# Seven block products for eight: Strassen's algorithm in the last block of a transformer layer

## The chip, the cores and the metric

The kernel runs on one core of a Trainium2 chip. The time is that of one execution on the device in microseconds. Comparisons use the median of several runs; before the change it is 1405.76 us (three runs, 1405.62 to 1406.48).

## The reference: what is computed

One pre-norm transformer layer on 2048 tokens of 512 features, in float32: attention with 32 query heads of 16 features that share one key and one value head, then a gated feed-forward part with 1792 hidden features.

```python
h  = x + A(layernorm(x))        # q = x@wq, k = x@wk, v = x@wv; softmax(q k^T / 4) v, all heads; @ wo
h2 = h + (gelu(n @ w_gate) * (n @ w_up)) @ w_down      # n = layernorm(h)
```

The change concerns the two products `n @ w_gate` and `n @ w_up`, each 512 x 512 by 512 x 1792 for a block of 512 tokens.

## The kernel before, in words

**Blocks and chunks.** The tokens are four blocks of 512 (`NB`, `T`). A block's dense part (`dense`) is the output projection, the layer norm, the feed-forward part and the residual sums. The hidden features are 14 chunks of 128 (`FC`). The dense part of block b runs between the attention steps of block b + 1 (`weave`, steps of the kind "woven"); that of the last block has no attention left beside it and runs alone, by `tail`, at the end. This last stretch is where most of the change lies.

**High and low parts.** TensorE multiplies in a format that keeps fewer bits than float32 (`F32R`). So each operand is split into a high part and a low rest (`split`: one copy, one subtraction), and each product is three matmuls: high by high, high by low, low by high. The split weights are made once, at the start of the kernel, by GpSimd (`part_weights`) and kept in device memory (`w1_d`, `w2_d`); a load of one chunk of `w_gate` or `w_up` brings both parts, 512 KB (`load_w1`), into one of `W1` buffers. Loads of `w_down` for two chunks are 1 MB (`load_w2`) and go to a ring of three.

**The last block.** `start_tail` makes the normalised input, transposed by TensorE (`x_turn`), as `xT_hi` and `xT_lo` (tiles `x2h`, `x2l`). For each chunk `up` runs 12 matmuls of 512 columns for the gate (`pg`) and 12 for the other factor (`pu`). VectorE evicts them and makes square and cubic term (`leave_gate`: tiles `g`, `ga`), ScalarE does the tanh (`gate`), VectorE multiplies and splits the result into `gh` and `gl`. After four chunks, `down` multiplies them by `w_down` for four token tiles of 128 (`pd`, 12 matmuls each) and VectorE adds each into `h` (`add_down`). Two chunks lie between the fourth chunk and its down product:

```python
RUNS = ((0, 1, 2, 3), (4, 5, 6, 7), (8, 9, 10, 11), (12, 13))
```

**What sets the order.** Every engine works through its own instructions in order. In the last stretch TensorE, ScalarE and GpSimd keep the order in which the code issues them; a scheduler places those of VectorE and the DMAs of the SP queue, once, when the program is built. An instruction waits for the semaphores of those it depends on, and all behind it on its engine wait too.

Of the kernel before, what the change touches and what calls it, by code (L numbers as in the profile page):

```python
# [9 lines left out]
F32 = mybir.dt.float32  # L10
# [9 lines left out]
P = 128  # L20
# [5 lines left out]
BOUND_PAD = 1.02  # L26
PB = 5

W1 = 6

W2 = 3

# [35 lines left out]
def kernel(  # L68
# [104 lines left out]
    def run(outer, first):  # L173
# [10 lines left out]
        def psum1(name):  # L184
            return ps.tile([P, T], F32, tag="d", bufs=width, name=name)
# [282 lines left out]
                step()  # L468

        def evacuate(b, g, acc):  # L470
            oT = sb.tile([P, T], F32, tag="oT", bufs=2, name=f"oT_{b}_{g}")
            nc.vector.tensor_copy(oT, acc)  # L472
            c, k = divmod(g, 2)
            last = b == NB - 1 and g == NG - 1
# [72 lines left out]
        def part_weights(pw):  # L547
# [53 lines left out]
                yield 1  # L601
            left()

        def load_w1(b, i):
# [53 lines left out]

        tail_ps = None

        def tail_bank(name):
# [12 lines left out]
        def dense(b, tail=False):  # L674
# [13 lines left out]
            w1 = {i: load_w1(b, i) for i in range(W1)}  # L688
            if b == 0:
                yield 0  # L690
            w2 = {}
# [16 lines left out]

            def x_turn(t):

                bank = tail_bank if tail and t != 2 else psum1
                pt = bank(f"pxt_{b}_{t}").rearrange("p (c q) -> p c q", c=DC)
                for c in range(DC):
                    nc.tensor.transpose(pt[:, c, :], xns[t][:, c * P : (c + 1) * P], ident)  # L714
# [32 lines left out]

            def start_tail():

                xp, xn, h = (  # L750
                    sb.tile([P, TB, D], F32, tag="p", bufs=PB, name=f"{n}p_{b}")
                    for n in ("x", "xn", "h")
                )
                for t in range(TB):
                    nc.sync.dma_start(xp[:, t, :], x_t[:, b * TB + t, :])
# [2 lines left out]
                nc.gpsimd.tensor_copy(one, ident)  # L758
                xh = sb.tile([P, TB, D], F32R, tag="p", bufs=PB, name=f"xhp_{b}")
                xl = sb.tile([P, TB, D], F32R, tag="p", bufs=PB, name=f"xlp_{b}")  # L760
                for t in range(TB):
# [61 lines left out]
            gs, g_of = {}, {}  # L823

            def next_w1(i):
                if i + W1 < 2 * FC:
                    w1[i + W1] = load_w1(b, i + W1)

            def leave_gate(f, pg):
# [36 lines left out]
            def up(f):  # L866
# [14 lines left out]
                for k in range(2):  # L881
                    next_w1(2 * f + k)
                yield CUT

            def up_plan(f, k):
                def terms():
# [125 lines left out]


            plan, prev = [], None
            for fs in RUNS:
                for n, f in enumerate(fs):
                    if tail:
                        yield from up(f)
                    else:
                        plan.extend(up_plan(f, k) for k in range(2))  # L1020
                    if tail and fs is RUNS[-1] and n == 0:
                        w2[f // 2] = load_w2(b, f // 2)
                    if tail and n == 1 and prev is not None:
                        yield from down(prev, False)
                    if tail and n == 1 and fs is not RUNS[-1]:
                        for g in fs[::2]:
                            w2[g // 2] = load_w2(b, g // 2)
                    if not tail and n == 1 and prev is not None and fs is not RUNS[-1]:
# [3 lines left out]
            if not tail:  # L1032
                yield from weave(plan)
                yield from down(RUNS[-2], False)
                load_wo(b + 1)
            yield from down(RUNS[-1], True)

        PER = NG * KC
# [16 lines left out]
        def open_gates():  # L1055
            while gates:
                gates.pop(0)()
# [132 lines left out]
            ["long"] * 4 + ["gap"] + ["woven"] * 6 * len(SIZES) + ["long"] * 4 + ["short"] * 2  # L1190
        )
        todo = list(kinds)
        fixed = ExitStack()
# [410 lines left out]
```

## Time and profile before

| what | us |
|---|---|
| median of the runs | 1405.76 |
| profiled execution, its time | 1405.77 |
| profiled execution, its span (first to last instruction) | 1404.1 |
| last block's products: first matmul of chunk 0 | from 1282.75 |
| TensorE's last matmul ends | about 1398.25 |
| TensorE busy, share of the span | 99% |
| GpSimd busy, share of the span | 15% |

A page of the profile gives each engine's busy time (PE is TensorE, PEld its weight loads, DVE VectorE, ACT ScalarE, POOL GpSimd, SP the queue of most DMAs), the busy shares in 40 equal slices, the chain of waits that ended last, and groups of instructions: line, engine, operation, output and inputs, shapes and count, then busy time in us and mean ns of one, then the idle time before them. A row of one line's instructions gives shortest, median and longest duration in ns. A row of the timeline gives start, busy time and count. Line numbers such as L669 are those of the kernel that ran; in the rows of the changed program they are those of the changed kernel.

### The profile page before, as it was taken

Reading aid. Unit: us, or ns where it says so; the run is one execution under the profiler, and the core shown is the slowest. Engines: PE = TensorE matmul, PEld = TensorE weight load, DVE = VectorE, ACT = ScalarE, POOL = GpSimd, SP = SyncE. Lnnn points to the kernel's source line nnn. Section 1 sums busy time; section 2 is a strip of 40 time slices with the busy share of each in tenths; the row PEclk is TensorE's granted clock in tenths of the full one; section 3 lists DMA queues with packets and bytes.
Section 4 is the critical chain, followed back from the end, with each engine's and each line's share of the span. In section 5 each row is a group of like instructions: output and inputs, shape, how many; then the busy total and the mean of one; then the engine's idle time right before and its main releaser. Section 6 shows DMA issues by size and latency. Waiting matters only on the chain.

```text
span 1404.1 us, 25676 instructions
## 1 busy us (share of the span) xinstructions
PE 1389.0 (99%) x10652; PEld 781.5 (56%) x10652; DVE 551.2 (39%) x983; ACT 1041.5 (74%) x1149; POOL 215.2 (15%) x327
## 2 busy tenths in 40 slices
PE   8999999999999999999999999999999999999998
PEld 7533333335565556555555555555555555557886
DVE  7322333323342424333252433424252342427665
ACT  7799999997777877877777777777787777772000
POOL 6588877101000000001000000001000000002000
PEclk9999999999999999999999999999999999999999
DMA  4578888532441423033242333034242241335550
GB/s 160 159 255 258 256 279 244 179 110 95 133 147 54 140 88 117 28 125 139 89 165 73 121 114 117 28 100 146 95 156 93 88 147 57 132 126 196 181 199 33
DMA packets 70189, 190.33 MB, mean 136 GB/s; under 512 B 10568, under 2 KB 10568, under 8 KB 70032
## 3 DMA queue, kind: packets, MB, share of 16 engines
q1 hardware_dynamic: 58856, 151.02, 32.8%
q0 software_dynamic: 10464, 36.43, 8.1%
q8 instruction: 86, 1.41, 0.4%
q10 hardware_dynamic: 744, 1.15, 0.2%
q14 instruction: 39, 0.32, 0.1%
HBM read 142.94 MB, written 45.35 MB: 134 GB/s over the span
## 4 chain that ended last, share of the span: by engine, by line
PE 94%; ACT 3%; DMA 1%; issue 0%; POOL 0%; DVE 0%; SPq 0%; ACTq 0%; DVEq 0%; POOLq 0%
PE acc L459 33%; PE s L451 19%; PE pu L970 9%; PE pg L970 8%; PE pd L970 5%; PE pq L449 4%; PE pd L647 3%; PE pd L669 3%; PE pg L669 3%; PE pu L669 3%; ACT p L455 3%; PE pp L647 2%; DMA x<-in_A_x_dram 1%; PE pp L778 1%; PE pxt L714 1%; PE pq L228 0%
## 5 line engine op out<-in xcount | busy, mean ns | idle before, releaser
L455 ACT ACTIVATE p<-s 128x1024 f32<-128x1024 f32 x1024 | 969.6, 1029 | 222.9 <-PE s L451 218.4
L459 PE MATMUL acc<-p,v_sb 128*32 128x512 f32 x4096 | 494.7, 598 | 0.0
L451 PE MATMUL s<-qg,kaug 50*128 50x512 f32 x1984 | 415.8, 423 | 3.8 <-ACT p L455 3.7
L451 PEld LDWEIGHTS s<-qg,kaug 50*128 50x128 f32 x1984 | 194.3, 184 | 218.5 <-ACT p L455 121.0
L459 PEld LDWEIGHTS acc<-p,v_sb 128*32 128x32 f32 x4096 | 109.8, 109 | 228.2 <-issue 225.4
L970 PE MATMUL pu<-x2h,w 64*128 64x512 f32 x672 | 211.7, 391 | 0.0
L970 PE MATMUL pg<-x2h,w 64*128 64x512 f32 x672 | 211.2, 391 | 0.0
L970 PEld LDWEIGHTS pu<-x2h,w 64*128 64x128 f32 x672 | 115.9, 185 | 14.8
L970 PEld LDWEIGHTS pg<-x2h,w 64*128 64x128 f32 x672 | 116.1, 185 | 13.1 <-DVE g L844 0.2
L970 PE MATMUL pg<-x2l,w 64*128 64x512 f32 x336 | 122.0, 391 | 0.0
L970 PE MATMUL pu<-x2l,w 64*128 64x512 f32 x336 | 122.0, 391 | 0.0
L144 POOL TENSOR_SCALAR rstd<-mv 128x1 f32<-128x1 f32 x16 | 3.6, 222 | 666.3 <-DVE mv L142 666.2
L847 ACT ACTIVATE ga<-ga 128x512 f32<-128x512 f32 x56 | 35.3, 634 | 89.4 <-DVE ga L842 89.4
L970 PE MATMUL pd<-w,gh 64*128 64x512 f32 x384 | 81.2, 392 | 0.0
L912 DVE TENSOR_TENSOR h<-h,pd 128x512 f32<-128x512 f32 x48 | 31.8, 684 | 115.4 <-PE pd L970 66.3
L1224 DVE SCALAR_TENSOR_TENSOR ga<-ga,g 128x512 f32<-128x512 f32 x70 | 48.4, 691 | 52.2 <-ACT ga L847 51.2
L472 DVE COPY oT<-acc 128x512 f32<-128x512 f32 x32 | 22.1, 692 | 111.4 <-PE acc L459 111.2
L499 DVE RECIPROCAL oc<-oc 128x128 f32<-128x128 f32 x64 | 56.3, 921 | 21.7 <-DMA oc<-acc_d 15.5
L831 DVE COPY g<-pg 128x512 f32<-128x512 f32 x56 | 38.7, 692 | 63.3 <-PE pg L970 57.6
L970 PEld LDWEIGHTS pu<-x2l,w 64*128 64x128 f32 x336 | 57.9, 185 | 7.2
L970 PEld LDWEIGHTS pg<-x2l,w 64*128 64x128 f32 x336 | 58.0, 185 | 6.8
L844 DVE SCALAR_TENSOR_TENSOR g<-g,pu 128x512 f32<-128x512 f32 x56 | 38.3, 684 | 40.2 <-PE pu L970 30.3
(276 smaller groups left out, 1492.3 us busy)
## 6 DMA issues: line engine op xcount, KB each, us to landing
w<-w_d SPq DMA_DIRECT2D x112, 512.0 KB
w<-w_d SPq DMA_DIRECT2D x28, 1024.0 KB
wo<-wo_d SPq DMA_DIRECT2D x8, 1024.0 KB
acc_d<-oT SPq DMA_DIRECT2D x31, 256.0 KB
oc<-acc_d SPq DMA_DIRECT2D x124, 64.0 KB
w_d<-w_0b POOLq DMA_DIRECT2D x14, 512.0 KB, 6.2
w_d<-w_1b POOLq DMA_DIRECT2D x14, 512.0 KB, 4.7
qg<-q_d SPq DMA_DIRECT2D x46, 128.0 KB
```

Of the source, the lines that this page charges most:

```text
L449: step()
L451: nc.tensor.matmul(s[:, a, :], kaug[rows, kc * P : (kc + 1) * P], qg[rows, 2 * u + a, :], start=True, stop=True,)
L455: nc.scalar.activation(p[:, 2 * u : 2 * u + 2, :], s, AF.Exp, scale=SCALE)
L459: nc.tensor.matmul(acc[32 * j : 32 * j + 32, :], v_sb[:, kc, :], p[:, j, :], start=(kc == 0), stop=(kc == KC - 1), skip_group_check=True,)
L499: nc.vector.reciprocal(oc[:, 1, sl], oc[:, 1, sl])
L647: nc.tensor.matmul(banks[k], lhsT[rows], rhs[rows], start=(turn == 0 and i == 0), stop=(turn == 1 and i == n - 1), skip_group_check=True,)
L669: nc.tensor.matmul(bank, lhsT, rhs, start=(i == 0), stop=(i == len(ts) - 1))
L831: nc.vector.tensor_copy(g, pg)
L844: nc.vector.scalar_tensor_tensor(g, g, 0.5, pu, op0=ALU.mult, op1=ALU.mult)
L847: nc.scalar.activation(a, a, AF.Tanh, scale=GELU_A * GELU_C)
L970: nc.tensor.matmul(e["bank"], lhsT[rows], rhs[rows], start=i == 0 and not e["both"], stop=last and e["both"], skip_group_check=True,)
L1224: (soon or lazy).pop(0)()
```

## The change

Chunks 2 to 11 of the last block are taken two at a time: five pairs (`SEVEN` holds their numbers, pair n has the chunks 2 SEVEN[n] and the next). For a pair, each of `w_gate` and `w_up` is a 256 x 512 block (as the product needs it), the input a 512 x 512 block, and both are cut into 2 x 2 parts: the weights into 128 features by 256, the input into 256 features by 256 tokens. Strassen's algorithm, in Winograd's form, gives the four parts of the result from seven part products instead of eight, each of a sum of weight parts by a sum of input parts.

- **Weights** (`seven_weights`). In the attention part of the program, one half unit of work at each "woven" step, GpSimd loads parts of `w_gate` and `w_up`, makes the combinations, splits each of seven into high and low and stores them to `ws_d`. There are 20 units; a unit has one load, five operations for the combinations, seven splits of two operations and seven stores of 128 KB, all on 128 x 128 tiles.
- **Input** (`differences`). After chunk 0 is issued, GpSimd adds `xT_hi` and `xT_lo` to float32 again (four operations) and makes four differences; ScalarE and VectorE split these into `t_hi` and `t_lo`.
- **Products** (`seven`). A product is 12 matmuls of 256 columns, for gate and other factor side by side in one bank of PSUM. The products 1, 6, 5 and 3 of a pair add up in one bank (`pa`), 7 and 4 in another (`pb`), 2 stands alone (`pc`). ScalarE copies the bank `pa` to memory after 1, 6 and 5 (`copy`, tiles `s`), before the next product adds to it; VectorE adds such a copy to another bank (`out_of`). `TURNS` gives the place of each product; the pairs overlap, and the down products and chunks 12 and 13 (`up_half`) are put between them.
- **After the products** (`activate`), for 128 features by 256 tokens each: GpSimd makes square and gate product, VectorE the cubic term, ScalarE the tanh and, new, the high part, VectorE the rest. The last two steps are issued three and four turns later.
- **Room.** Weight buffers 5 instead of 6, `oT` one instead of two, and the last block's PSUM banks in two groups: three ("t") and two ("b"), where five ("t") were; the transposes take the two.

```diff
-W1 = 6
+W1 = 5
+SEVEN = (1, 2, 3, 4, 5)
+TURNS = {1: 0, 7: 2, 6: 4, 2: 5, 5: 6, 3: 8, 4: 10}
+DOWN_AT = ((14, 16, 18, 20), (28, 30, 32, 34))
+HALF = 256
...
+    ws_d = dram.tile([len(SEVEN), 8, P, 2, 2, 2, P], F32R, name="ws_d")
...
-            oT = sb.tile([P, T], F32, tag="oT", bufs=2, name=f"oT_{b}_{g}")
+            oT = sb.tile([P, T], F32, tag="oT", bufs=1, name=f"oT_{b}_{g}")
...
+                def leave(j, src):
+                    part = db.tile([P, 2, P], F32R, tag="s_p", bufs=3, name=f"sp_{n}_{k}_{c}_{j}")
+                    split(nc.gpsimd, part[:, 0], part[:, 1], src, nc.gpsimd)
+                    nc.gpsimd.dma_start(ws_d[n, j, :, k, c].bitcast(F32), part.bitcast(F32))
+                leave(1, a11)
+                leave(2, a12)
+                nc.gpsimd.tensor_scalar(t, a22, -1.0, None, op0=ALU.mult)
+                leave(4, t)
+                yield
+                nc.gpsimd.tensor_tensor(t, a21, a22, op=ALU.add)
+                leave(5, t)
+                nc.gpsimd.tensor_tensor(t, t, a11, op=ALU.subtract)
+                leave(6, t)
+                nc.gpsimd.tensor_tensor(t, a12, t, op=ALU.subtract)
+                leave(3, t)
+                nc.gpsimd.tensor_tensor(t, a11, a21, op=ALU.subtract)
+                leave(7, t)
+                if i + 1 < len(units):
+                    raw = load(*units[i + 1])
+                yield
...
-            return tail_ps.tile([P, T], F32, tag="t", bufs=5, name=name)
+            return tail_ps.tile([P, T], F32, tag=tag, bufs={"t": 3, "b": 2}[tag], name=name)
...
-                bank = tail_bank if tail and t != 2 else psum1
+                bank = partial(tail_bank, tag="b") if tail and t != 2 else psum1
...
+            def differences():
+                for h in range(2):
+                    for cols in (second, first):
+                        nc.gpsimd.tensor_tensor(
+                            halves(x32, h, cols), halves(xT_hi, h, cols).bitcast(F32),
+                            halves(xT_lo, h, cols).bitcast(F32), op=ALU.add,
+                        )
...
+                for k, one, two in (
+                    (3, b22, b12), (1, b12, b11), (2, b22, ts[:, 0]), (4, ts[:, 1], b21)
+                ):
+                    nc.gpsimd.tensor_tensor(ts[:, k - 1], one, two, op=ALU.subtract)
+                    split(nc.scalar, t_hi[:, k - 1], t_lo[:, k - 1], ts[:, k - 1])
...
+                def activate(f, half, y):
+                    nc.gpsimd.tensor_tensor(a, g, g, op=ALU.mult)
+                    nc.vector.scalar_tensor_tensor(
+                        a, a, 1.0 / GELU_A, g, op0=ALU.add, op1=ALU.mult
+                    )
+                    nc.gpsimd.tensor_tensor(u, g, u, op=ALU.mult)
...
+                    slow.append([3, gate])
+                    slow.append([4, leave])
...
+                    product(n, j, bank, j in (1, 7, 2))
+                    if j in (1, 6, 5):
+                        copy(n, j, bank)
...
+            if tail:
+                yield from up(0)
+                ts = differences()
+                yield from up(1)
+                seven(*ts)
+                yield from down(RUNS[2], False)
+                yield from down(RUNS[3], True)
+                return
...
+            if kind == "woven" and seven_parts is not None:
+                next(seven_parts, None)
```

**How it moves the order.** First place: ScalarE at the start of the last block's products. In the rows a tile's name ends with its own number; `hp` are the residual sums, `ga_0` and `ga_1` the tanh arguments of chunks 0 and 1. Before:

```order
L819 ACTIVATE hp_13471<-pp_2_13498 128x512
L819 ACTIVATE hp_13471<-pp_3_13499 128x512
L847 ACTIVATE ga_0_13703<-ga_0_13703 128x512
L847 ACTIVATE ga_1_13745<-ga_1_13745 128x512
L847 ACTIVATE ga_2_13789<-ga_2_13789 128x512
```

The changed program, same engine and place; `s_0_1` is the copy after product 1 of pair 0:

```order
L889 ACTIVATE hp_14198<-pp_2_14217 128x512
L889 ACTIVATE hp_14198<-pp_3_14218 128x512
L919 ACTIVATE ga_0_14422<-ga_0_14422 128x512
L138 ACTIVATE t_hi_14437<-ts_14443 128x512 x4
L919 ACTIVATE ga_1_14484<-ga_1_14484 128x512
L1074 ACTIVATE s_0_1_14515<-pa_0_14500 128x512
L1074 ACTIVATE s_0_6_14546<-pa_0_14500 128x512
```

Four splits have come between the two tanh, and the copies of the bank follow the tanh of chunk 1.

Second place: VectorE at the same time. Before:

```order
L880 SCALAR_TENSOR_TENSOR ga_0_13703<-ga_0_13703,g_0_13701 128x512
L880 CAST gh_0_13708<-ga_0_13703 128x512
L880 TENSOR_TENSOR gl_0_13709<-ga_0_13703,gh_0_13708 128x512
L831 COPY g_1_13743<-pg_1_13717 128x512
L842 TENSOR_TENSOR ga_1_13745<-g_1_13743 128x512
L842 SCALAR_TENSOR_TENSOR ga_1_13745<-ga_1_13745,g_1_13743 128x512
```

The changed program:

```order
L141 TENSOR_TENSOR t_lo_14438<-ts_14443,t_hi_14437 128x512
L952 SCALAR_TENSOR_TENSOR ga_0_14422<-ga_0_14422,g_0_14420 128x512
L141 TENSOR_TENSOR t_lo_14438<-ts_14443,t_hi_14437 128x512
L952 CAST gh_0_14427<-ga_0_14422 128x512
L141 TENSOR_TENSOR t_lo_14438<-ts_14443,t_hi_14437 128x512
L952 TENSOR_TENSOR gl_0_14428<-ga_0_14422,gh_0_14427 128x512
L141 TENSOR_TENSOR t_lo_14438<-ts_14443,t_hi_14437 128x512
L903 COPY g_1_14482<-pg_1_14456 128x512
L914 TENSOR_TENSOR ga_1_14484<-g_1_14482 128x512
L914 SCALAR_TENSOR_TENSOR ga_1_14484<-ga_1_14484,g_1_14482 128x512
```

The four low parts stand between the steps of chunk 0 and ahead of the eviction of chunk 1.

Third place: ScalarE before the last down products, where `a_11_0` is chunk 11, first half of the tokens. The changed program:

```order
L1050 ACTIVATE a_10_1_15343<-a_10_1_15343 128x256
L1061 ACTIVATE gh_10_15347<-a_10_1_15343 128x256
L919 ACTIVATE ga_13_15412<-ga_13_15412 128x512
L1050 ACTIVATE a_11_0_15391<-a_11_0_15391 128x256
L1061 ACTIVATE gh_10_15347<-a_11_0_15391 128x256
```

Before, the tanh of chunk 11 stood two places ahead of that of chunk 13; now half of it stands behind, and chunk 11's high part with it.

More of the change, by code (lines that the diff above doesn't have):

```diff
@@ L748, in start_tail @@
             def start_tail():
-                xp, xn, h = (
+                xp, xn = (
                     sb.tile([P, TB, D], F32, tag="p", bufs=PB, name=f"{n}p_{b}")
-                    for n in ("x", "xn", "h")
+                    for n in ("x", "xn")
                 )
@@ L883, in up, with up_half @@
                 yield CUT
+            def up_half(i):
+                f, k = divmod(i, 2)
+                hi, lo = w1.pop(i)
+                terms = [(w[:, c, :], xT_hi[:, c, :]) for c in range(DC) for w in (hi, lo)]
+                terms += [(hi[:, c, :], xT_lo[:, c, :]) for c in range(DC)]
+                bank = tail_bank(f"p{'gu'[k]}_{b}_{f}")
+                for n, (lhsT, rhs) in enumerate(terms):
+                    nc.tensor.matmul(
+                        bank, lhsT, rhs, start=(n == 0), stop=(n == len(terms) - 1)
+                    )
+                load_row()
+                (leave_up if k else leave_gate)(f, bank)
+                open_gates()
+                while lazy:
+                    lazy.pop(0)()
@@ L1014, in dense @@
             plan, prev = [], None
+            if tail:
+                yield from up(0)
[5 more added lines that the diff above has]
+                return
             for fs in RUNS:
                 for n, f in enumerate(fs):
[L1017 to L1028, printed above, removed]
+                    plan.extend(up_plan(f, k) for k in range(2))
+                    if n == 1 and prev is not None and fs is not RUNS[-1]:
                         tw = []
@@ L1031, in dense @@
                 prev = fs
[L1032 to L1035, printed above, removed]
+            yield from weave(plan)
+            yield from down(RUNS[-2], False)
+            load_wo(b + 1)
             yield from down(RUNS[-1], True)
@@ L1192, in run @@
         todo = list(kinds)
+        seven_parts = seven_weights() if first else None
         fixed = ExitStack()
```

171 lines of the change are left out of this document (168 added, 3 removed).

## The prediction

> **What bounds the kernel now.** I read the page first, then the chain of waits of the last 122 us, then the rows of the instructions that the change multiplies.
>
> ```profile
> span 1404.1 us, 25676 instructions
> PE 1389.0 (99%) x10652; PEld 781.5 (56%) x10652; DVE 551.2 (39%) x983; ACT 1041.5 (74%) x1149; POOL 215.2 (15%) x327
> POOL 6588877101000000001000000001000000002000
> PE 94%; ACT 3%; DMA 1%; issue 0%; POOL 0%; DVE 0%; SPq 0%; ACTq 0%; DVEq 0%; POOLq 0%
> ```
>
> TensorE carries 94% of the chain and GpSimd (POOL) is free from about 280 us on. The profiled execution took 1405.77 us, 1.67 us above its span; the median of the runs shown is 1405.76, so the sum is made on 1405.77.
>
> The chain over the last block's dense part (start, length, what):
>
> ```profile
> 1282.75 2.95 PE pg L669 x12
> 1285.70 2.72 PE pu L669 x12
> 1315.62 11.16 PE pd L669 x48
> 1381.48 16.75 PE pd L669 x72
> 1398.25 0.69 DVE hp L912
> ```
>
> From 1282.75 to 1398.25 TensorE never waits. Twelve matmuls of 512 columns take 2.72 us, 227 ns each; the down product takes 11.16 / 48 = 232 ns each. Here every TensorE microsecond saved or lost is one at the end.
>
> **The products.** Ten chunks of two products now cost 10 x 5.44 = 54.4 us. After: five pairs of chunks, seven products each, 12 matmuls of 256 columns per product: 420. No row has such a matmul; its price is bounded by these (the loads in the first answer are those of the first two matmuls of 1282.68):
>
> ```profile
> 1282.68 0.30 PEld L669 LDWEIGHTS pg<-x2h,w 128*128 128x128 f32 x2 [0.37 <-ACT x2h L816]
> L669 PEld LDWEIGHTS pg<-x2h,w x112: 186/188/189, 1282.7 to 1377.2; 128*128 128x128 f32 x112
> 1280.76 1.09 PE L714 MATMUL pxt<-ident,xnp 128*128 128x128 f32 x8
> L714 PE MATMUL pxt<-ident,xnp x16: 270/273/330, 1277.2 to 1281.6; 128*128 128x128 f32 x16
> ```
>
> Two loads of 188 ns cover only 300 ns, so the second began 112 ns after the first: a load holds its path 112 ns, and a pair cannot go faster than that. From the other side, 227 ns for 512 columns is at most 113 ns for half of them if nothing is fixed, and more with a fixed part. The small transposes show a load and its matmul following each other at (1.09 - 0.27) / 7 = 117 ns. I take 120 ns, between 113 and 128. If loads could not overlap at all it would be 188. So 420 x 0.120 = 50.4 us: **-4.0 us** (113: -6.9; 128: -0.6). The arithmetic alone saves an eighth, 6.8 us; part of it is lost because the load no longer hides under the matmul with room to spare.
>
> The Trainium skill, "TensorE: Matmul & The Clock Gate", section "LDWEIGHTS (loading the stationary operand)", gives columns / 1.2 ns, 107 ns for 128 columns: with the isolated gap of the section before it, 109 ns for 256 columns, the estimate would be about 110 ns and -8.2 us. The trace's 227 ns against that page's 216 for 512 columns says a fixed part is paid here; the row decides.
>
> **The seam, where the preparation is late.** GpSimd rebuilds the normalised input from its two parts (four operations at L988) and forms four differences (L998), each 128 x 512; ScalarE and VectorE split each into high and low (L138, L141). The front shows what that does to both queues: on VectorE the four `t_lo` stand ahead of the eviction of chunk 1, and on ScalarE the tanh of chunk 1 stands ahead of the copy `s_0_1`. Product 6 of the first pair accumulates into the bank that this copy must first have read (`pa_0`). So TensorE waits for: eight GpSimd operations, a split, chunk 1's evictions, its tanh, the copy. The durations:
>
> ```profile
> L135 POOL TENSOR_TENSOR xlp<-xp,xhp 128x512 fp32r<-128x512 f32 x4 | 5.1, 1292 | 282.1 <-ACT xhp L132 282.1
> 1280.93 2.47 DVE L816 TENSOR_TENSOR x2l<-pxt,x2h 128x512 fp32r<-128x512 f32 x4
> 1285.73 0.69 DVE L831 COPY g<-pg 128x512 f32<-128x512 f32 x1 [1.14 <-PE pg L669]
> 1289.97 0.43 DVE L880 CAST gh<-ga 128x512 fp32r<-128x512 f32 x1
> 1287.91 0.63 ACT L847 ACTIVATE ga<-ga 128x512 f32<-128x512 f32 x1 [4.39 <-DVE ga L842]
> ```
>
> First, a small loss: the four transposes now share two banks, so the fourth waits until VectorE has read the first (first quarter of the 2.47 us, 1281.55) instead of starting near 1281.2: **+0.5 us** (0 to 1), and all below moves with it. TensorE then does chunks 0 and 1 (2.95 + 3 x 2.72 = 11.11 us) and two products (2 x 1.44) and wants product 6 at 1282.75 + 0.5 + 11.11 + 2.88 = 1297.2.
>
> GpSimd starts at 1283.40 + 0.5 = 1283.9 and needs eight times 1.29 us plus some 0.08 between: 11.0 us, 1294.9. Meanwhile VectorE does operations of two SBUF operands, for which these rows show a price (the first and third from 60 to 230 us, where GpSimd is busy, the second and fourth from 300 to 900, where it is idle):
>
> ```profile
> L514 DVE TENSOR_TENSOR o_lo<-oc,o_hi 128x512 fp32r<-128x512 f32 x2 | 2.5, 1233 | 0.0
> L514 DVE TENSOR_TENSOR o_lo<-oc,o_hi 128x512 fp32r<-128x512 f32 x8 | 5.5, 688 | 0.1
> L472 DVE COPY oT<-acc 128x512 f32<-128x512 f32 x5 | 3.5, 691 | 31.0 <-PE acc L459 31.0
> L472 DVE COPY oT<-acc 128x512 f32<-128x512 f32 x15 | 10.4, 692 | 41.8 <-PE acc L459 41.8
> L135 POOL TENSOR_TENSOR w_1b<-w_1b x14: 1267/1284/1602, 80.6 to 246.9; 128x512 fp32r<-128x512 f32 x14
> ```
>
> Operations between SBUF tiles stretch from 0.69 to 1.23 us beside a busy GpSimd, and GpSimd's from 1.28 to 1.60; reads of PSUM don't. Beside the eight operations stand six such of 0.69 and a cast of 0.43, 4.6 us. Of these I let half fall into the chain, 2.3 (ends 0 and 4.6): 1297.2. Then split 0.63, low part 0.69, eviction, square and cubic 3 x 0.69, tanh 0.63, copy 0.63 and some 0.25 between them: 4.9, to 1302.1. **Stall 4.9 us** (2.6 to 7.2). The cover that would hide it, chunks 0 and 1, is used up.
>
> The Trainium skill, "SBUF — State Buffer", section "Who interferes with whom", calls the port that VectorE's second operand shares with GpSimd an exclusive lock. By that rule the whole 4.6 us would be served one after the other and the stall be 7.2; the rows agree with the sign, and don't show how much falls into the chain.
>
> **The clock.** The last rows of the trace, after TensorE has ended (stretch, length, busy times, granted clock):
>
> ```profile
> 1398.00:1401.00 3.00, 0.21 (x1) 0.00 (x0) 0.69 (x1) 0.00 (x0) 0.00 (x0) 1.00 0.53 190
> 1401.00:1402.00 1.00, 0.00 (x0) 0.00 (x0) 0.00 (x0) 0.00 (x0) 0.00 (x0) 0.82 0.03 10
> 1402.00:1403.00 1.00, 0.00 (x0) 0.00 (x0) 0.00 (x0) 0.00 (x0) 0.00 (x0) 0.50 0.00 0
> ```
>
> TensorE's last matmul ends near 1398.25; 0.82 over 1401 to 1402 means a drop to half at 1401.64, after 3.4 us idle. A stall of 4.9 us is long enough. If the clock takes as long to come back, 3.4 us run at half speed and 1.7 are lost; I book **+1.5** (0 if the stall stays under 3.4; 3.5 if twice as long).
>
> **Between.** Per product one 512 KB load of weights, 35 in place of 20. Rate and size:
>
> ```profile
> w<-w_d SPq DMA_DIRECT2D x112, 512.0 KB
> 1286.00:1290.00 4.00, 4.00 (x19) 3.34 (x18) 3.22 (x6) 0.63 (x1) 0.00 (x0) 1.00 0.98 358
> ```
>
> At 98% of the engines' time 358 GB/s moved, 1.46 us for a load against 1.44 for a product: level. Five buffers hold 7.2 us of products. After the first down product SP issues two down-weight loads (2 MB, 5.9 us) ahead of the next products' loads, while seven products run on end: 5.9 + 1.46 against 7.2 and some latency, **+1.0** (0 to 3). PSUM copies (three of 0.63 on ScalarE per pair), four evictions of 0.69, and half-width gate work fit into a pair's 10 us on each engine: nothing, as long as no copy is late; that is a rival.
>
> **The end.** After the last up product TensorE goes straight to the down products of chunks 8 to 11 and needs chunk 11's first half after nine matmuls, 2.1 us. Its tanh stands behind that of chunk 13 on ScalarE (front). From the end of chunk 13's last product: VectorE finishing what is queued 0.7, eviction, square, cubic 2.2, tanh 0.66, half tanh, product, high part some 0.45 each: 5.0. **Stall 2.9** (0.2 if the eviction of chunk 13's gate, ready 2.72 us earlier, is done in time; 4). In the kernel before, chunk 11 is finished two chunks earlier.
>
> **The attention part.** GpSimd's 20 units there (7 splits and 5 combinations of 128 x 128, 8 DMAs) are work off TensorE's path, at
>
> ```profile
> L135 POOL TENSOR_TENSOR o_lo<-oc,o_hi x4: 460/464/466, 1270.9 to 1276.3; 128x128 fp32r<-128x128 f32 x4
> L564 POOL DMA_DIRECT2D w_d<-w_1b x14 | 7.7, 552 | 0.3 <-POOL w_1b L135 0.3
> L451 PE MATMUL s<-qg,kaug 50*128 50x512 f32 x1984 | 415.8, 423 | 3.8 <-ACT p L455 3.7
> ```
>
> about 7 + 8 x 0.55 = 12 us per unit, beside two steps of the schedule. What it can cost is VectorE's delay of at most 0.46 us an operation. TensorE's idle time over all score products is 3.8 us, although GpSimd was 80% busy in slices 2 to 7: **+0.3** (0 to 3). The smaller rings (5 for 6 weight buffers, one `oT`) have loads of 1.5 us against steps of several: nothing; if a load were late, its whole 2 us.
>
> **Sum**: -4.0 + 0.5 + 4.9 + 1.5 + 1.0 + 2.9 + 0.3 = +7.1, so 1405.77 + 7.1 = 1412.9, given as 1413.0.
>
> **The rivals.** (a) *The preparation costs no port time.* If GpSimd and VectorE don't delay each other, the seam's stall is 2.6, under the 3.4 us that the clock needs, and the end about 0.5: -4.0 + 0.5 + 2.6 + 0.5 + 0.5 = +0.1, 1405.9; with 113 ns a further 2.9 less, 1403.0, faster only below that. It decides when the eight operations end before 1295. For it: GpSimd's median of 1284 ns barely moves beside VectorE; against: VectorE's 1233. (b) *Late copies all along.* Each pair has two places where the next product waits for ScalarE's copy of the same bank one product earlier; 0.4 us late at ten of them is +4: 1417. For it: ScalarE now also waits for GpSimd's squares in between; against: 10 us of work per engine has room. (c) *The loads bound the stretch.* At 300 GB/s a load takes 1.75 us, 0.3 over a product in the some fourteen products without cover: +4, 1417. (d) *Weights do not pipeline*: 188 ns a pair, 28.6 more, 1441; the 300 ns row speaks against it. That fewer products are done than announced is excluded: the order has 84 matmuls of 256 columns per pair.
>
> **How the numbers follow.** Forecast 0.55 (its own range 1409 to 1416.5), (a) 0.20, (b) 0.13, (c) 0.08, (d) 0.04. Differences under 0.2%, 2.8 us, cannot be told from no change: faster is below 1402.9, and same up to 1408.6. Of (a) I give 0.07 to faster and 0.13 to the same; all the others are slower, 0.80. The range 1407 to 1420 leaves out most of (a), (d) and the ends.
>
> **What would show it.** Twelve-matmul rows of 1.44 us in the chain; one idle stretch of TensorE before `pa_0` near 1297, released by ScalarE, with a granted clock below 1 behind it; one before `pd` near the end. A seam stall under 3 us or a product under 1.36 us would make it wrong downwards, idle time before most products upwards.

## The result

| | median, us | lowest to highest | runs |
|---|---|---|---|
| before | 1405.87 | 1405.32 to 1406.48 | 6 |
| after | 1465.79 | 1464.26 to 1468.60 | 6 |

The ratio is 1.0428 (95% interval 1.0414 to 1.0441): the changed kernel is 60 us slower. The prediction said 1413, 1407 to 1420. The profiled execution took 1468.6 us, 2.8 more than the median; the changed kernel varies more from run to run than the kernel before.

The page of the changed kernel, its first parts:

```profile
span 1466.8 us, 26894 instructions
PE 1393.2 (95%) x10832; PEld 791.1 (54%) x10832; DVE 563.9 (38%) x997; ACT 1061.0 (72%) x1198; POOL 516.5 (35%) x915
PE   8999999999999999960999999999999999998987
POOL 6587876015666566655540000000000000014330
PEclk9999999999999999985999999999999999999999
PE 67%; POOL 11%; DMA 9%; issue 7%; DVE 3%; ACT 2%; SPq 0%; POOLq 0%; ACTq 0%; DVEq 0%
```

TensorE is busy for as long as before (1393 us for 1389), so it idles some 58 us longer. The hole is not in the last block but in slices 18 and 19 of 40, near 650 us. GpSimd, nearly idle there before, is busy from 340 to 760 us. It has 11% of the chain of waits, and the loads and stores that it asks for have most of the DMA's 9%.

TensorE's waits in the changed kernel (engine, line, what it waited for: us in total, times, longest), then the end of the long one in the timeline:

```profile
PE pxt L783 <- DVE xn L797: 46.4, 1, 46.4
PE pa L1023 <- ACT s L1074: 4.4, 1, 4.4
PE pc L1023 <- DMA ws<-ws_d: 4.2, 1, 4.2
PE pd L719 <- ACT gh L1061: 1.3, 1, 1.3
PE pxt L783 <- DVE x2l L886: 0.3, 1, 0.3
693.80 1.12 PE L783 MATMUL pxt<-ident,xn 128*128 128x128 f32 x4 [46.42 <-DVE xn L797]
```

One wait of 46.4 us: the transposes at the start of block 1's dense part wait for VectorE's normalised rows `xn`. VectorE was not late itself: it waited 50.4 us for GpSimd's `rstd`. The same place on VectorE and on GpSimd:

```profile
693.19 0.55 DVE L797 TENSOR_SCALAR xn<-h,mv,rstd 128x512 f32<-128x512 f32 x1 [50.40 <-POOL rstd L151]
691.59 0.61 POOL L630 DMA_DIRECT2D ws_d<-sp  x1 [0.30 <-POOL sp L141]
692.28 0.22 POOL L150 TENSOR_SCALAR rstd<-mv 128x1 f32<-128x1 f32 x1
```

`rstd` is the reciprocal root of the layer norm, two operations on GpSimd of under 1 us each (`layer_norm`, used by `residual`). GpSimd takes its instructions in order, and ahead of block 1's roots stand 17.5 units of the weights' preparation. At 647.4, when TensorE wants the rows, GpSimd has more than two of them still to do. Each microsecond of that backlog is one of TensorE, and the chain of waits runs through it.

How long a unit takes is read from GpSimd's groups between 342 and 664 us, in which 16 units ran (busy us and mean ns, then the idle time before them and what ended it):

```profile
L630 POOL DMA_DIRECT2D ws_d<-sp x112 | 63.5, 567 | 35.1 <-POOL sp L141 32.9 <-issue 2.1
L141 POOL TENSOR_TENSOR sp<-st,sp 128x128 fp32r<-128x128 f32 x80 | 38.8, 485 | 6.5
L140 POOL CAST sp<-st 128x128 fp32r<-128x128 f32 x80 | 24.7, 309 | 8.5 <-DMA ws_d<-sp 3.7
L141 POOL TENSOR_TENSOR sp<-sr,sp 128x128 fp32r<-128x128 f32 x32 | 16.3, 510 | 2.7
L140 POOL CAST sp<-sr 128x128 fp32r<-128x128 f32 x32 | 12.4, 388 | 58.2 <-DMA sr<-in_B_w_up_dram 32.8 <-DMA sr<-in_B_w_gate_dram 25.4
```

Per unit: splits (38.8 + 24.7 + 16.3 + 12.4) / 16 = 5.8 us, five combinations 2.7 (rows of 16 with 7.9 to 9.6 us each), stores and load issued 4.7, the wait before each store for the split just ahead of it 35.1 / 16 = 2.2, the wait for the raw weights 58.2 / 16 = 3.6, small gaps 1.1. Together 20 us. A unit had (647.4 - 342.4) / 17.5 = 17.4.

The last block's part of the chain, start, length and what:

```profile
1333.22 2.96 PE pg L719 x12
1341.67 1.11 DVE t_lo L141
1342.78 1.70 DVE ga L952
1344.48 1.71 DVE t_lo L141
1346.52 0.60 DVE t_lo L141
1350.95 0.59 ACT s L1074
1351.58 2.93 PE pa L1023 x12
1354.51 2.56 PE pc L1023 x12
1364.58 1.44 PE pa L1023 x12
1391.52 9.85 DMA ws<-ws_d
1401.41 2.44 PE pc L1023 x12
1403.85 3.62 PE pa L1023 x24
1459.40 0.69 DVE hp L1170
```

From 1333.22 to 1459.40 are 126.2 us, where the kernel before took 115.5 (1282.75 to 1398.25): 10.7 longer. So of the 61.1 us by which TensorE ends later, 50 lie ahead of the last block's dense part and 11 in it or just ahead of it; some 1.6 more come after TensorE's end, in the last stores. What divides the two parts in the runs below is the last exponential of the attention, whose start is the last number but the shape in these rows (before, after):

```profile
L455 ACT ACTIVATE p<-s x1024: 1015/1026/1123, 49.9 to 1261.6; 128x1024 f32<-128x1024 f32 x171
L461 ACT ACTIVATE p<-s x1024: 1012/1026/1127, 49.9 to 1311.6; 128x1024 f32<-128x1024 f32 x171
```

"Attention part" below is the time to that point, 50.0 us more than before; "end part" is from there to VectorE's last `hp`, 147.8 us for 136.6.

### The profile page after: what moved, and what is told of

It reads as the page before. It is cut to its first block, busy times and chain, and to the rows that moved or that the text cites. A ratio compares the mean times of both kernels' runs of the same rounds, so it can differ in the third digit from the quotient of the medians.

```text
span 1466.8 us, 26894 instructions
## 1 busy us (share of the span) xinstructions
PE 1393.2 (95%) x10832; PEld 791.1 (54%) x10832; DVE 563.9 (38%) x997; ACT 1061.0 (72%) x1198; POOL 516.5 (35%) x915
## 3 DMA queue, kind: packets, MB, share of 16 engines
q8 instruction: 87, 1.43, 0.4%
q10 hardware_dynamic: 744, 1.15, 0.2%
## 4 chain that ended last, share of the span: by engine, by line
PE 67%; POOL 11%; DMA 9%; issue 7%; DVE 3%; ACT 2%; SPq 0%; POOLq 0%; ACTq 0%; DVEq 0%
PE acc L465 24%; PE s L457 13%; PE pu L1228 6%; PE pg L1228 5%; PE pq L455 4%; POOL sp L141 4%; PE pd L1228 3%; DMA sr<-in_B_w_up_dram 3%; POOL sp L140 3%; DMA sr<-in_B_w_gate_dram 3%; DMA ws_d<-sp 2%; PE pa L1023 2%; PE pd L697 2%; POOL ws_d L630 2%; PE pd L1128 2%
## 5 line engine op out<-in xcount | busy, mean ns | idle before, releaser
L141 POOL TENSOR_TENSOR xlp<-xp,xhp 128x512 fp32r<-128x512 f32 x4 | 5.1, 1294 | 282.1 <-ACT xhp L138 282.1
L630 POOL DMA_DIRECT2D ws_d<-sp x140 | 79.5, 568 | 43.4 <-POOL sp L141 41.3
L1170 DVE TENSOR_TENSOR h<-h,pd 128x512 f32<-128x512 f32 x48 | 31.8, 684 | 115.5 <-PE pd L1228 66.4
L1480 DVE SCALAR_TENSOR_TENSOR ga<-ga,g 128x512 f32<-128x512 f32 x70 | 50.4, 721 | 52.0 <-ACT ga L919 51.0
L903 DVE COPY g<-pg 128x512 f32<-128x512 f32 x46 | 31.7, 689 | 56.2 <-PE pg L1228 54.2
```

Of the source, the lines that this page charges most:

```text
L141: (eng_lo or nc.vector).tensor_tensor(lo, src, hi.bitcast(F32), op=ALU.subtract)
L630: nc.gpsimd.dma_start(ws_d[n, j, :, k, c].bitcast(F32), part.bitcast(F32))
L903: nc.vector.tensor_copy(g, pg)
L1170: nc.vector.tensor_tensor(hs[t], hs[t], pd, op=ALU.add)
L1480: (soon or lazy).pop(0)()
```

## The experiments

First question: is the attention part's loss the backlog in GpSimd's queue, or the load that the preparation puts on ports and DMA engines? Four kernels. All but the last keep the changed last block.

**Half a unit at every second step.**

```diff
-            if kind == "woven" and seven_parts is not None:
+            if kind == "woven" and seven_parts is not None and c % 2 == 0:
                 next(seven_parts, None)
```

> The half units of the weights' preparation are put into GpSimd's queue at every second woven step, so that they reach into the third block instead of the second; nothing else differs from the changed kernel. Theory 'queue': TensorE's one stall of 46.4 us is block 1's normalisation, whose reciprocal root stands in GpSimd's in-order queue behind 17.5 units that take 20.0 us each (342.4 to 692.3 us) where a unit has two steps' time, about 14; at half the rate a unit has about 28 us and no backlog forms. The stall goes and with it the slow clock behind it: the last block's dense part began 50.5 us late (1333.2 for 1282.7), so 1465.8 - 50.5 = 1415, 1413 to 1418, and the rest of the loss is the 10.7 us of the last block's dense part. Rival 'contention': the preparation's 280 stores, loads and port use slow TensorE's feeders wherever they lie; then moving them only moves the loss, and the time stays above 1430.

Measured: 1417.35 us, ratio 1.0084 (1.0067 to 1.0100). The stall is gone; the attention part is 2.1 us longer than before. But the reason in the expectation, the rate, was wrong, as GpSimd's row at block 1's roots shows:

```profile
642.78 0.22 POOL L150 TENSOR_SCALAR rstd<-mv 128x1 f32<-128x1 f32 x1 [131.09 <-DVE mv L148]
```

GpSimd waited 131 us there for VectorE. The steps do not pace it: it does what stands in its queue at full speed and then waits at the next root. The place of a unit in the program only decides which roots it stands ahead of; here 8.5 units stood ahead of block 1's.

**The same rate, with six steps left free before the block's end.**

```diff
-            if kind == "woven" and seven_parts is not None:
+            if kind == "woven" and seven_parts is not None and (b > 0 or todo.count("woven") >= 6):
```

> The preparation keeps its rate of one half unit per woven step, but the last six woven steps of the first block are left free and the remaining half units follow in the second block. Theory 'queue': at 20.0 us a unit the 14.5 units ahead of block 1's reciprocal roots are done at 342.4 + 14.5 x 20.0 = 632, before 647 when TensorE wants the normalised rows, so the stall is gone: 1415, as with half the rate. Theory 'contention' (the rate of the preparation is what hurts): no better than a tenth of the loss, 1455 or more. Were it the preparation's unit length under load that grows, a stall of some us stays.

Measured: 1418.74 us, 1.0098 (1.0081 to 1.0114), no stall: block 1's root is reached with 11.8 us to spare. Three units fewer ahead of the root are enough, at an unchanged rate. That excludes contention as the main cause.

**The raw weights asked for one unit ahead.**

```diff
-                raw = db.tile([P, 2, HALF], F32, tag="s_raw", bufs=1, name=f"sr_{n}_{k}_{c}")
+                raw = db.tile([P, 2, HALF], F32, tag="s_raw", bufs=2, name=f"sr_{n}_{k}_{c}")
...
+                raw, ahead = ahead, load(*units[i + 1]) if i + 1 < len(units) else None
...
-                    part = db.tile([P, 2, P], F32R, tag="s_p", bufs=3, name=f"sp_{n}_{k}_{c}_{j}")
+                    part = db.tile([P, 2, P], F32R, tag="s_p", bufs=2, name=f"sp_{n}_{k}_{c}_{j}")
```

> Same places in the queue as the changed kernel, but each unit's 256 KB of raw weights are asked for one unit ahead (two raw buffers; the differences are formed in place and two buffers instead of three hold the parts, to make room). Theory 'queue, unit mis-sized': a unit is 20.0 us because 2.9 us of waiting for the load, a load that is asked for only when the unit before it is done, stand in it each time. Without that wait a unit is 17.2 and the 17.5 units end at 342.4 + 17.5 x 17.2 = 643 to 648: the stall falls from 46.4 to between 0 and 4 us, 1415 to 1420. If a unit is bound by its stores' landing (two buffers) or by GpSimd beside a busy VectorE, it stays near 19 and 30 us of the stall with it: 1445.

Measured: 1441.17 us, 1.0259 (1.0242 to 1.0277). Near the last case of the expectation, between the two. TensorE's long wait, then GpSimd's two between 342 and 664 us:

```profile
PE pxt L781 <- DVE xn L795: 18.1, 1, 18.1
POOL sp L140 <- DMA ws_d<-sp: 35.6, 27, 4.0
POOL sp L140 <- DMA sr<-in_B_w_gate_dram: 1.7, 1, 1.7
```

The wait for raw weights fell from 58.2 to 1.7 us and the stall from 46.4 to 18.1. But with two buffers for the parts instead of three, 35.6 us of waiting for the stores came in place of 3.7. A unit took (663.7 - 342.5) / 17.5 = 18.4 us: the stall follows the unit's length, 17.5 times 1.6 us shorter being 28 us.

**The preparation alone**, on the kernel before, its last block unchanged.

> The kernel before with only the preparation of the weights added, at the places where the changed kernel has it, and with its smaller rings (five weight buffers, one oT); what is prepared is not used, and the last block's products stay as they were. Theory 'queue': the preparation alone costs 46.4 us of stall and some 4 us of slow clock and others behind it: 1405.9 + 50.5 = 1456, 1452 to 1459. If instead the changed last block (its buffers and loads, which a scheduler may order differently) had a part in it, less: 1406 if the preparation is harmless.

Measured: 1455.45 us, 1.0350 (1.0333 to 1.0368), with the same stall:

```profile
PE pxt L757 <- DVE xn L771: 46.5, 1, 46.5
```

So 49.9 of the 59.9 us belong to the preparation alone (with the smaller rings that make room for it). Its end part is as before (last exponential at 1312.0, last `hp` at 1448.6: 136.6).

Second question: what the end part's waits are made of. These three kernels stand on the first of the experiments (half a unit at every second step), whose end part is 147.1 us. Five traces have this last block unaltered, and its end part is 145.2 to 147.8 us in them; the wait for `ws`, 2.8 to 4.2 us, differs most. So a difference of less than some 3 us between two single traces tells nothing.

**The copy ahead of the tanh.** In `up`, chunk 1's gate is not opened; it is opened after the first product, behind the copy `s_0_1`:

```diff
-                open_gates()
-                while lazy:
-                    lazy.pop(0)()
+                if f != 1:
+                    open_gates()
+                    while lazy:
+                        lazy.pop(0)()
...
                     step()
+                    open_gates()
+                    while lazy:
+                        lazy.pop(0)()
...
```

> On the kernel with the preparation at every second step: the tanh of chunk 1, and what follows it, is put behind the copy s_0_1 on ScalarE instead of ahead of it; nothing else. There the stall before product 6 of the first pair is 4.37 us (1299.37 to 1303.75), and the copy's own inputs are long there: product 1 has ended near 1297.8 and the fourth t_hi on ScalarE at 1298.47. Theory 'tanh ahead of the copy': the copy then ends near 1299.1, the stall falls under 1 us, and with it goes the slow clock behind it (2.93 for 1.44 us of the next product): 1417.4 - 4.4 - 1.9 = 1411, 1409 to 1413. Rival 'the differences are late': were GpSimd's eight operations with their splits what is waited for, the stall would stay at 3 us or more and no more than 1.5 be won.

Measured: 1415.55 us (1412.53 to 1419.34), 1.0067 (1.0048 to 1.0085), against 1.0084: by the times alone not told apart, and above the range expected. The trace tells it. The wait, and the granted clock where it stood (stretch, length, busy time of PE, PEld, DVE, ACT, POOL with counts, clock, DMA share, GB/s), here and in the kernel that it is built on:

```profile
PE pa L1024 <- ACT s L1075: 1.4, 1, 1.4
1304.00:1306.00 2.00, 1.34 (x11) 1.34 (x12) 1.83 (x4) 0.60 (x2) 0.00 (x0) 1.00 0.91 289
```

```profile
PE pa L1023 <- ACT s L1074: 4.4, 1, 4.4
1303.00:1305.00 2.00, 1.25 (x6) 1.26 (x7) 1.83 (x4) 0.69 (x2) 0.00 (x0) 0.54 0.13 53
```

The stall ahead of product 6 is gone, so the copy waited for the tanh on ScalarE and not for the differences; these only made the tanh late, since VectorE makes their low parts ahead of its input. But the next copy, `s_0_6`, now stands behind that tanh and is waited for 1.4 us; a down product waits 0.8 us for chunk 1's low part. The clock stays full, and the end part is 4.3 us shorter (142.8), where I had expected 6.3.

**One down load later.**

```diff
+W2_AT = 27
...
-                                w2_of = RUNS[run + 2][0] // 2
-                                w2[w2_of] = load_w2(b, w2_of)
+                                if run:
+                                    w2[6] = load_w2(b, 6)
+                    if at == W2_AT:
+                        w2[4] = load_w2(b, 4)
```

> On the kernel with the preparation at every second step: of the two down weights of 1 MB that SP asks for after the first run's down products, the second, which is needed only at the end, is asked for seven turns later. Theory 'burst': the one wait of a product on its weights (3.7 us before pc of the fourth pair, with a slow clock behind it: 2.93 and 4.29 us for 1.44 and 2.88) comes from 2 MB ahead of the products' loads in one queue; with 1 MB less ahead, 2.5 us at 412 GB/s, and 1 MB at another place, the stall is under 1.3 and does not reach the clock: 1417.4 - 3.7 - 2.9 + 1 = 1412, 1410 to 1414. Rival 'the loads bound the stretch as a whole' (one 512 KB load per product of 1.44 us): the stall only moves to a later product, and less than 2 us are won.

Measured: 1413.46 us, 1.0057 (1.0042 to 1.0073). No product of the pairs waits for its weights any more (chunk 13 waits 0.8 us for its own), and the end part is 140.7 us, 6.4 shorter (the profiled executions differ by 6.1 us, the medians by 3.9). The cause of this wait is the burst: 2 MB ahead of the products' loads in one queue. That the loads bound the whole stretch falls for this kernel; the last kernel below shows how little room they have.

**Both.**

> Both edits of the two other runs at once, on the kernel with the preparation at every second step. If the two stalls are independent, the gains add: 1417.4 - 6.3 - 5.6 = 1405.5, 1403 to 1408, which is the time of the kernel before: what seven products for eight save (4.0 us) is then given back by the 1.3 us wait for chunk 11 near the end, the 2 us that the preparation still costs in the attention part, and 0.5 around the transposes. If the first stall gave the loads the time to run ahead, the second grows when it goes, and the sum is worse than its parts: 1408 or more.

Measured: 1411.06 us, 1.0045 (1.0031 to 1.0058), end part 138.0: 9.1 us shorter, where the two alone give 4.3 + 6.4 = 10.7. They nearly add, and the rival of the expectation, a longer wait for the loads, does not show (0.3 us). The total is above the range expected because of the attention part: 5.4 us longer than before, although its code is that of the runs with 2.1, 3.0 and 3.4. All four lose at one place, at 378 to 390 us: 4.3 us here, 1.5, 1.3 and 2.4 in the others. SP's four loads of the attention's result there and VectorE's reciprocal, before first, then in this run:

```profile
374.54 1.72 SPq L485 DMA_DIRECT2D oc<-acc_d  x4
378.18 1.76 DVE L499 RECIPROCAL oc<-oc 128x128 f32<-128x128 f32 x2 [2.38 <-DMA oc<-acc_d]
```

```profile
376.48 1.74 SPq L492 DMA_DIRECT2D oc<-acc_d  x4
381.94 1.77 DVE L506 RECIPROCAL oc<-oc 128x128 f32<-128x128 f32 x2 [6.18 <-DMA qg<-q_d]
PE pg L1235 <- DVE g L917: 2.4, 1, 2.4
```

The attention's result goes through device memory (`acc_d`) to change its layout; beside the preparation's stores the way out takes 1.9 us longer (the loads wait for it) and the way back as much again (the wait is put down to the loads issued next to it). VectorE's reciprocal waits for it, the evictions stand behind the reciprocal, and TensorE waits for an eviction.

**All of it.** Preparation at every second step from the eighth on; chunks 12 and 13 ahead of the products, their down products first at the end; chunk 13's tanh behind `s_0_1`; one down load later.

```diff
...
-                yield from up(0)
-                ts = differences()
-                yield from up(1)
-                seven(*ts)
-                yield from down(RUNS[2], False)
-                yield from down(RUNS[3], True)
+                yield from up(0)
+                yield from up(1)
+                yield from up(12)
+                ts = differences()
+                yield from up(13)
+                seven(*ts)
+                yield from down(RUNS[3], False)
+                yield from down(RUNS[2], True)
...
```

> The seven products with every loss that the runs have named worked on at once: preparation at every second step and only from the eighth woven step on (VectorE's first evictions of the dense part waited 1.3 us beside it); chunks 12 and 13 computed ahead of the products, so that the differences have 10.9 us more cover and the last down products begin with chunks 12 and 13 instead of waiting for chunk 11; chunk 13's tanh behind the copy s_0_1; the 1 MB load of the down weights of chunks 12 and 13 seven turns later. From the kernel before: -4.0 for the products, +0.5 for the transposes, +0.5 to 1 for the preparation, up to 1 for what stays of the stalls: 1405.5 - 2 = 1403.5, 1401.5 to 1406. If the stalls come from a shortage of an engine or of the loads as a whole and not from the order, they come back elsewhere: 1409 or more.

Measured: 1408.27 us (11 runs, 1407.21 to 1410.58), 1.0019 (1.0010 to 1.0028), above the 1401.5 to 1406 expected. The waits between the last exponential and the end, and the last exponential:

```profile
PE pd L720 <- DVE hp L1176: 0.6, 1, 0.6
PE pb L1026 <- DVE t_lo L142: 0.6, 1, 0.6
PE pxt L782 <- DVE x2l L885: 0.4, 1, 0.4
L462 ACT ACTIVATE p<-s x1024: 1013/1026/1122, 49.9 to 1264.0; 128x1024 f32<-128x1024 f32 x171
1399.11 0.69 DVE hp L1176
```

The end part is 135.1 us: for the first time shorter than before, by 1.5 us, in this one execution. The attention part is 2.4 longer. Starting later in the queue did not help there, since GpSimd runs ahead: the stores are at 380 us all the same.

**The preparation in the second and third block**, two half units in three steps: once on the changed kernel, once on the last one.

```diff
-            if kind == "woven" and seven_parts is not None:
+            if kind == "woven" and seven_parts is not None and b > 0 and c % 3 < 2:
```

> The changed kernel with one edit: the preparation's half units stand at two of three woven steps of the second and third block instead of at every one of the first block. GpSimd runs ahead of the other engines, so what counts is how many units stand ahead of a block's reciprocal roots: none ahead of block 1's, 11.5 ahead of block 2's, 230 us of the 300 there are. Theory 'queue': no stall, as with the other two placements. The second claim tested: those two lost a further 1 to 5 us at one place, 380 to 390 us, where VectorE's reciprocal waited 4.1 to 6.2 us for its numerator, which comes back through DRAM, instead of 2.4, while the preparation's stores ran; without them there the exponentials end within 0.7 us of the kernel before (2.1 in the run at every second step): 1417.4 - 1.5 = 1416, 1414.5 to 1417.5. If the loss follows the preparation into the second block, it stays at 1417 to 1420.

> The kernel of the run 'best' with its preparation moved to the same places, the second and third block. There the dense part and its end came out 1.6 us shorter than in the kernel before (135.05 for 136.61 us from the last exponential to TensorE's end), and the attention part 2.4 us longer, nearly all of it at 380 to 390 us. With that loss gone: 1405.9 - 1.6 + 0.5 and some 0.5 that the last stores take longer = 1405.3, 1404 to 1407. If the loss comes back in the second block: 1408.

Measured: 1418.51 us, 1.0093 (1.0078 to 1.0109), and 1407.56 us (11 runs, 1405.29 to 1408.89), 1.0009 (1.0000 to 1.0018). In both the first block is as before to 0.1 us, so the loss at 380 us did come from the preparation beside it (though not every time: with the raw weights asked for ahead, the preparation runs there too and nothing is lost). But it does not simply vanish: the attention part ends 1.0 and 1.7 us late, lost now in steps of 0.2 to 1.2 us in the later blocks (in the second kernel at 789 and 1152 us). Both times are above the ranges expected, the first by 1 us, the second by 0.6. And the end part of the second kernel, whose last block is that of the run before, is not 135.1 us in its profiled execution but 137.2 (last exponential at 1263.3, last `hp` at 1400.5), 0.6 longer than before the change, for two products wait for their weights again:

```profile
PE pc L1026 <- DMA ws<-ws_d: 1.1, 1, 1.1
PE pa L1026 <- DMA ws<-ws_d: 0.9, 1, 0.9
```

In this execution the loads had no room left, and that the end part gains at all is not shown. The second kernel, with every named loss worked on, cannot be told from the kernel before.

## Why the prediction was wrong

**The step that failed is the attention part**, "+0.3 (0 to 3)", "work off TensorE's path". It measured 50.0 us: 46.4 of stall, some 2.5 lost at half speed behind it (the granted clock is 0.50 from 694 to 698 us), 1.1 at 380 us and after. Two errors stand in it.

The unit was mis-sized: "about 7 + 8 x 0.55 = 12 us" for 20. The operations were 8.5 for 7, the issues 4.7 for 4.4; what was left out is the wait of each store for the split ahead of it (2.2), and the wait for the raw weights (3.6), which the diff itself shows, one buffer whose load is asked for when the unit before is done.

The larger error is the question not asked. The prediction named ports as the only thing that GpSimd's work could cost, and did not name what stands behind it on GpSimd. Two small operations of the next block's layer norm do, and through VectorE all of TensorE waits for them. With 12 us a unit the backlog would have been done by 342.4 + 17.5 x 12 = 552, and the step would have been right by luck; the margin was 5.4 us a unit and was never worked out. "Beside two steps of the schedule" took the steps to pace GpSimd, which they do not.

The Trainium skill, "DMA: Bandwidth & Descriptors", section "Anatomy of one DMA — SWDGE (gpsimd) path", gives about 2.0 us plus bytes / 436e3 for a transfer that GpSimd asks for. For these 256 KB the estimate would be 2.6 us. The trace has a median of 3.5 from issue to landing (3.0 to 8.3), with 0.73 for the issue itself. With a wait of 2.6 the unit would have come out near 15, still under 17.4.

**The last block** was predicted at +6.8 and took +10.7 from its first matmul on and 0.3 ahead of it. Term by term:

| term | predicted | measured |
|---|---|---|
| products | -4.0 | -4.0 (1.44 us each) |
| transposes' bank | +0.5 | +0.3 |
| seam stall | +4.9 | +4.4 |
| slow clock behind it | +1.5 | +2.9 |
| loads | +1.0 | +5.9 |
| end stall | +2.9 | +1.3 |

*Products*: the taken 120 ns held; it was a choice within 113 to 128. The Trainium skill's estimate of 110 ns ("TensorE: Matmul & The Clock Gate", section "LDWEIGHTS (loading the stationary operand)") did not: twelve matmuls take 1.43 to 1.45 us, 120 ns each, wherever a product follows another at full clock.

*Seam*: place and releaser are as predicted, and the experiment shows the tanh ahead of the copy as the decider. The size came out near (4.4 for 4.9), in part by luck. Of the 2.3 us booked for GpSimd and VectorE delaying each other, GpSimd's eight operations lost only 0.9 (11.87 us, from 1333.77 to 1345.64, for 11.0). But from there to the end of the copy it took 5.9 us for 4.9, because VectorE had work left over: its three operations of 1.11, 1.70 and 1.71 us take 0.60 to 0.70 when GpSimd is idle, 2.6 us lost together. The stall of 7.2 that the prediction worked out from the Trainium skill's exclusive lock ("SBUF — State Buffer", section "Who interferes with whom") did not come. But the lock itself fits the trace: each of the five VectorE operations of two SBUF operands that meet one of GpSimd's ends 0.54 or 0.55 us after it, and each of the four GpSimd operations that meet one of VectorE's already under way ends 1.15 or 1.16 after that. They take turns; only part of VectorE's 4.6 us met GpSimd's work at all.

*Clock*: 2.93 + 2.56 + 4.63 us for products worth 7.2, so 2.9. The prediction let half speed last 3.4 us, as long as the clock takes to fall; it lasted 6.1 us.

*Loads*: the mechanism was right (2 MB of down weights ahead of the products' loads), the size was off, 4.2 us of stall and 1.7 of slow clock (2.44 and 3.62 for 1.44 and 2.88). The prediction let the loads land one after the other, 7.4 us after the first down weight is asked for; it took 12.7, from 1388.71 to 1401.37. The trace has sixteen completions for each load, and load by load they do come in turn: for the first down weight from 1393.34 to 1396.44, for the second from 1396.99 to 1400.08, for the load that is waited for from 1398.24 to 1401.37, for the next one from 1399.53 to 1402.65. Two things were left out of the sum. When the first down weight was asked for, the loads ahead of it were still under way, the last of them until 1391.69. And the last part of a load lands 3.1 us after its first part here, and the product waits for the last. What holds the late parts back is not shown.

*End*: place and releaser are as predicted. The path was shorter because VectorE began to evict chunk 13's gate 0.7 us before the last up product ended (at 1440.24), where 0.7 after it was booked.

*Rivals*: none of the four says what happened. (a), no delay between GpSimd and VectorE, falls by these delays, and (d), loads that do not overlap, by the 120 ns. Of (b) and (c), late copies and late loads all along, the changed kernel's trace shows nothing: each wait is one event.

## What to carry to other kernels

When work is added to an idle engine, read what already stands in that engine's queue behind the new work, when it is due and who waits for it; an engine that is 15% busy can still be the one that a layer norm waits for. Here it ran ahead until an instruction of its own had to wait (131 us at one root), so the program's steps set the order of its work and not its pace. And size the unit with its own waits (a load asked for only when the last unit is done, a store that waits for the operation ahead of it), because a backlog multiplies the error by the number of units.

## What was not expected of the hardware

A stall costs TensorE more than its length, and by how much varies. After 4.4 us of idle time the clock was at 0.50 for the next 6.1 us of work in the changed kernel (from 1351.58; a mean of 0.83 over 1357 to 1359 is half until 1357.7), and full again after 2.8 in the run with the preparation at every second step, at the same place (from 1303.75; a mean of 0.61 is half until 1306.6):

```profile
1355.00:1357.00 2.00, 2.00 (x11) 2.00 (x11) 0.00 (x0) 0.15 (x1) 0.00 (x0) 0.50 0.72 240
1357.00:1359.00 2.00, 2.00 (x16) 2.00 (x15) 1.10 (x2) 0.14 (x1) 1.05 (x2) 0.83 0.46 125
```

```profile
1305.00:1307.00 2.00, 2.00 (x13) 2.00 (x13) 0.32 (x1) 0.29 (x1) 0.00 (x0) 0.61 0.03 8
1307.00:1309.00 2.00, 2.00 (x19) 2.00 (x18) 0.69 (x1) 0.31 (x1) 0.00 (x1) 1.00 0.65 211
```

And every kernel with the preparation in it varies by 2 to 7 us between runs, the kernel before by about 1. That the stores of GpSimd's queue meet other transfers differently in each run, as at 380 us, would explain it; only one execution of each kernel has a trace, so it is argued and not shown.
